# Storing the first batch's g early and lending its place in SBUF to q and v of every second group of four heads

## The chip, the cores and the metric

The kernel runs on one core of a Trainium2 chip. The metric is the time of one execution on the device in microseconds (us), taken as the median of several runs. The profile shows one execution. Its engines are PE (TensorE, matmuls, and PEld for the loading of their weights), DVE (VectorE), ACT (ScalarE), POOL (GpSimd) and SP (SyncE, which here only issues transfers). DMA stands for the 16 engines that carry out the transfers.

## The reference, cut to what matters

```python
def reference(q, k, v, w_a, w_b, w_out, phi, w1, w2):   # q, k, v: (4, 12, 448, 64)
    scores = np.matmul(q, k.transpose(0, 1, 3, 2)) / np.sqrt(64) - np.log(448)
    x = np.matmul(1 / (1 + np.exp(-scores)), v)          # sigmoid attention
    x = x.transpose(0, 2, 1, 3).reshape(1792, 768)
    x = (x @ w_a) * (x @ w_b) @ w_out                    # g = (x @ w_a) * (x @ w_b): 1792 x 1536
    logits = x @ phi                                     # 1792 x 32
    d = softmax(logits, axis=0)                          # over the tokens
    c = softmax(logits, axis=1)                          # over the slots
    s = (d.T @ x).reshape(8, 4, 768)                     # 4 slots for each of 8 experts
    s = [np.maximum(s[e] @ w1[e], 0) @ w2[e] for e in range(8)]
    return c @ np.concatenate(s)
```

## The kernel before

The work is staged as follows. Attention runs over groups `g` of two heads, 24 in all, six to a batch. While PE works on the attention of the second batch, it also forms g of the first batch (`ab(0)`). Then comes the attention of the third and fourth batches alone (groups 12 to 23), with the preparation of the later operands between its steps. Next, g of the second and third batches is formed together in 12 units of seven matrix products (L826), and then g of the fourth batch (`ab(3)`). Last, the expert weights (`e<-in_moe_w`) are streamed in and the experts are computed.

From group `GQ` = 14 on, a head's 448 rows of keys are split into three chunks of 128 and a tail of 64. The tails of an even group and of the odd group behind it are done together, so groups 14 and 15, 16 and 17, 18 and 19, 20 and 21, 22 and 23 each make one group of four heads. For each group:

- SP loads k and q (four transfers each, L141) and v (two transfers, L150 and L151).
- VectorE transposes k (L179), casts it to a high part (L171), subtracts to get a low part (L172) and keeps the tail (L198), and then does the same with q. This is `emit_TK(g)`, and it stands in the program one group ahead of its use.
- PE forms the scores of a chunk in three thirds: high times high, low times high, high times low (L231). ScalarE takes the sigmoid (L237).
- PE multiplies by v (`emit_PV`, L266), and for an odd group also does the tails: their scores (L246) and their product with v (L273).
- The result is copied out (`emit_x`, L296).

Within the loop of group g the order on PE is: the scores of chunk 0 of group g, the product with v of group g-1, then the remaining scores of group g. Three places in SBUF for k, four for q and three for v serve all groups in turn.

The first batch's g is needed in token order for d.T @ g. For its first two thirds (`gi` 0 and 1) VectorE transposes blocks of 32 x 32 into `gk_01`, the result is stored to DRAM (`gk32`, `store_gk`, four transfers for each third, L615) and read back in token order (`reload_gk`, L629 and L630). In this kernel the generator `turn_0` does this late: it takes one step for each step of the attention loop once group 19 is done. The products of `dg` (L919) read what was reloaded.

The order on every engine is that of the program. SP issues its transfers strictly in order, so a transfer that has to wait for its place, or for another transfer, holds all behind it. `load_u` (L694) is a load of weights for the units; its data go through `prep_u`.

Of the kernel before, what the change touches and what calls it, by code (L numbers as in the profile page):

```python
# [9 lines left out]
F32 = mybir.dt.float32  # L10
# [8 lines left out]
B, H, S, D = 4, 12, 448, 64  # L19
DM, FF, NS, NE, F = 768, 1536, 32, 8, 1024  # L20
C = 4
# [9 lines left out]
GQ = 2 * NP + 2  # L31
# [5 lines left out]
def body(ctx, tc, q, k, v, w_a, w_b, w_out, phi, w1, w2, out):  # L37
# [17 lines left out]
    run = {}  # L55
# [22 lines left out]
    gk_01 = lgp.tile([128, 2, 2048], F32, name="gk_01")  # L78
# [38 lines left out]


    qkv_t = {}
    held = []  # L120

    def chunks_of(g):
        return (T, C) if g < GQ else (128, 3)
# [1 line left out]
    def load_qkv(g, names):  # L125
        if g >= B * NP:
            return
        if g > 2 * NP and "raws" not in run:
            held.append((g, names))
            return  # L130
        b, p = divmod(g, NP)
        for src, nm, n in ((k, "k", 3), (q, "q", 4), (v, "v", 3)):
            if nm not in names:
                continue

            t = atp.tile([128, 2 * C * D], F32, tag=nm + "n", name=nm + "n", bufs=n)
            if g >= GT0:
                if nm != "v":
                    t = t[:, :S].rearrange("p (n d) -> p n d", d=32)
                    for j in range(4):  # L140
                        sp.dma_start(out=t[32 * j:32 * j + 32],  # L141
                                     in_=src[b, 2 * p + j // 2][:, j % 2 * 32:j % 2 * 32 + 32].rearrange(
                                         "(n t) d -> t n d", t=32))
                elif g < GQ:
                    t = t[:T].rearrange("p (h c d) -> p h c d", h=2, c=C)
                    sp.dma_start(out=t, in_=src[b, 2 * p:2 * p + 2].rearrange("h (c p) d -> p h c d", c=C))
                else:
                    t = t.rearrange("p (h n) -> p h n", h=2)
                    s, r = src[b, 2 * p:2 * p + 2], 64 * (g % 2)
                    sp.dma_start(out=t[:, :, :192], in_=s[:, :384].rearrange("h (p c) d -> p h (c d)", c=3))  # L150
                    sp.dma_start(out=t[r:r + 64, :, 192:], in_=s[:, 384:].rearrange("h p d -> p h d"))  # L151
                    t = t.rearrange("p h (c d) -> p h c d", c=C)
                qkv_t[nm, g] = t
                continue
            s = src[b, 2 * p:2 * p + 2].rearrange(
                "h (c p) d -> p h c d" if nm == "q" else "h (p c) d -> p h c d", c=C)
            if nm == "v":
                t = t[:T].rearrange("p (h c d) -> p h c d", h=2, c=C)
                sp.dma_start(out=t, in_=s)
            else:  # L160
                t = t[:T].rearrange("p (c h d) -> p c h d", c=C, h=2)
                for h in range(2):
                    (sp if g or not h else act).dma_start(out=t[:, :, h], in_=s[:, h])
            qkv_t[nm, g] = t
# [23 lines left out]
    def emit_TK(g):  # L188
        if g >= B * NP:
            return  # L190
        if g >= GT0:
            for nm in "kq":
                t = transposed(g, nm)
                split_heads(g, nm, t, dve.tensor_copy)
                if g >= GQ:
                    if nm == "k":
                        kr = atp.tile([128, 64], F32, tag="kr", name="kr", bufs=3)
                        dve.tensor_copy(kr, t[:, 384:])  # L198
                        t = kr
                    whole[nm, g] = t  # L200
                if nm == "k" or g <= GQ:
                    load_qkv(g + 3, nm)
            return
        tk = transposed(g, "k")
        if not g:
            tq = transposed(g, "q")
        split_heads(g, "k", tk, dve.tensor_copy)
        if not g:
            split_heads(g, "q", tq, act.copy)
# [30 lines left out]
    def emit_S_rest(g):  # L240

        sc = [ms() for _ in range(2)]
        for d in range(2):
            for h in range(2):
                r, f = slice(64 * h, 64 * h + 64), 64 * d
                pe.matmul(sc[h][f:f + 64], whole["k", g - 1 + d][r], whole["q", g - 1 + d][r], start=True, stop=True)  # L246
        for h in range(2):
            sigmoid(g, h, 3, sc[h], 128)
        for d in range(2):
            del whole["k", g - 1 + d], whole["q", g - 1 + d]  # L250
            load_qkv(g + 3 + d, "q")

    pv_t = {}

# [35 lines left out]
    def emit_x(g):  # L290
        pv = pv_t.pop(g)
        qkv_t.pop(("v", g))
        b, kk = divmod(g, NP)
        if b:
            xt[g] = raw_x(b, kk)
            (dve.tensor_copy if g > GQ and g % 2 else act.copy)(xt[g], pv)  # L296
        else:
            xh = x0p.tile([128, S], F32R, tag=f"xh{kk}", name=f"xh{kk}")
            xl = x0p.tile([128, S], F32R, tag=f"xl{kk}", name=f"xl{kk}")
            act.activation(xh, pv, AF.Copy)  # L300
            dve.tensor_tensor(xl, pv, xh.bitcast(F32), op=ALU.subtract)
            xt[g] = (xh, xl)
        if g < GQ or g % 2 == 0:
            load_qkv(g + 3, "v")

    def att():

        emit_TK(0)
        yield 860
        for g in range(B * NP + 1):  # L310
            more = g < B * NP
            dense = g < NP or g >= 2 * NP
            first = ((0, 1) if g in (0, B * NP - 1) else (0,) if dense else ()) if more else ()
            if g:
                emit_TK(g + 1)
                if g > GQ + 1 and g % 2:
                    load_qkv(g + 1, "v")
                yield 430
            for c in first:
                emit_S(g, (c,))  # L320
                run["done"] = True
                yield 800
            if g:
                if g < NP and more:
                    emit_TQ(g + 1)
                    yield 430
                emit_PV(g - 1)
                if g <= GQ:
                    emit_x(g - 1)
                elif g % 2 == 0:  # L330
                    emit_x(g - 2)
                    emit_x(g - 1)
                yield 3200
            else:
                emit_TK(g + 1)
                yield 430
            if not more:
                return
            if not dense:
                emit_S(g, (0, 1))  # L340
                yield 1600
                emit_TQ(g + 1)
                yield 430
                emit_S(g, (2, 3))
                yield 1600
            else:
                if not g:
                    emit_TQ(g + 1)
                    yield 430
                for c in range(chunks_of(g)[1]):  # L350
                    if c not in first:
                        emit_S(g, (c,))
                        yield 800
                if g >= GQ and g % 2:
                    emit_S_rest(g)
                    yield 800
# [208 lines left out]
    def group(b, gi, evac=(act.copy, dve.tensor_copy) * 2):  # L565
# [12 lines left out]
        if gi < 2:  # L578
            turned = gk[:, :4 * S].rearrange("p (n f) -> p n f", f=128)
            for j in range(4):  # L580
# [3 lines left out]
                    yield  # L584
                gT.pop((b, 4 * gi + j))
                live.discard(b * KF + 4 * gi + j)
            if b:
                yield from store_gk(b, gi, turned)
            else:
                turned_0.append(turned)  # L590
            return
# [17 lines left out]

    turned_0 = []  # L610

    def store_gk(b, gi, turned):
        dst = gk32[b, gi].rearrange("(n t) (r f) -> r t n f", t=32, r=4)
        for r in range(4):
            (act if b == B - 1 else sp).dma_start(out=dst[r], in_=turned[32 * r:32 * r + 32])  # L615
            if b in (0, B - 1):
                yield

    def turn_0():
        for gi in range(2):  # L620
            yield from store_gk(0, gi, turned_0[gi])
        for gi in range(2):
            reload_gk(0, gi, gk_01[:, gi])
            yield

    def reload_gk(b, gi, t):
        t = t.rearrange("p (c n) -> p c n", c=C)
# [467 lines left out]
        next(bg)  # L1095

    base = att_state[0]
    for frac in ab(0):
        att_to(base + NP * PAIR * min(1.0, frac * 1.02))
    att_pairs(2 * NP)  # L1100
    for kk in range(NP):
# [2 lines left out]
    x0_ctx.close()  # L1104
    pools["cp"] = cp_ctx.enter_context(tc.tile_pool(name="cp", bufs=1, side="left"))
    run["lsd2"] = pools["cp"].tile([128, 2 * S + 2 * C * NS], F32, name="ls_d")
    ops, pu, t0 = operands(), None, turn_0()
    wait = [(15, 0), (17, 1)]
    for cost in att_g:
        if wait and wait[0][0] in xt:  # L1110
            load_u(wait.pop(0)[1])
        if 19 in xt:
            next(t0, None)
        if not run.pop("trans", False):
            fill_step()
        run.pop("done", None)
        if next(ops, 0) == 0:
            pu = pu or prep_u(0)
            next(pu, None)
        if (4 * NP - 1, 0, C - 1) in a_t:  # L1120
            break
    run.pop("exp")()
    for _ in t0:
        pass
    for _ in ops:
        pass
    for _ in pu or prep_u(0):
# [198 lines left out]
```

## Time and profile before

| what | value |
|---|---|
| median of 3 runs | 678.41 us (677.24 to 678.56) |
| the profiled execution's own time | 675.91 us |
| its span | 674.1 us |
| PE busy | 634.4 us (94% of the span) |
| DVE busy | 403.6 us (60%) |
| POOL busy | 307.6 us (46%) |
| ACT busy | 283.2 us (42%) |
| moved by DMA | 154.25 MB, 229 GB/s in the mean |

The span is what the profile covers, from the first to the last instruction; the execution's own time includes what lies around it. Busy times are sums over stages with different limits, so the table says how the engines stand to each other, and not which stage could be shorter.

### The profile page before, as it was taken

Reading aid. Unit: us, or ns where it says so; the run is one execution under the profiler, and the core shown is the slowest. Engines: PE = TensorE matmul, PEld = TensorE weight load, DVE = VectorE, ACT = ScalarE, POOL = GpSimd, SP = SyncE. Lnnn points to the kernel's source line nnn. Section 1 sums busy time; section 2 is a strip of 40 time slices with the busy share of each in tenths; the row PEclk is TensorE's granted clock in tenths of the full one; section 3 lists DMA queues with packets and bytes.
Section 4 is the critical chain, followed back from the end, with each engine's and each line's share of the span. In section 5 each row is a group of like instructions: output and inputs, shape, how many; then the busy total and the mean of one; then the engine's idle time right before and its main releaser. Section 6 shows DMA issues by size and latency. Waiting matters only on the chain.

```text
span 674.1 us, 10877 instructions
## 1 busy us (share of the span) xinstructions
PE 634.4 (94%) x4015; PEld 449.8 (67%) x4015; DVE 403.6 (60%) x578; ACT 283.2 (42%) x512; POOL 307.6 (46%) x236
## 2 busy tenths in 40 slices
PE   6999999999998998989999999999999998997585
PEld 4556777777765554559989898898879896442121
DVE  4676899999973889658876777754233323200013
ACT  4888778779644676653332223201110002110022
POOL 0243676676734247549996575742344442000000
PEclk9999999999999999999999999999999999998998
DMA  9998999998863487921123233341999999999998
GB/s 210 272 261 212 292 300 290 307 285 272 263 156 88 86 143 152 238 63 47 48 89 94 71 92 100 96 125 44 294 385 358 403 341 353 404 416 416 410 372 305
DMA packets 145396, 154.25 MB, mean 229 GB/s; under 512 B 74336, under 2 KB 121792, under 8 KB 142272
## 3 DMA queue, kind: packets, MB, share of 16 engines
q1 hardware_dynamic: 138768, 150.01, 72.1%
q10 hardware_dynamic: 6576, 3.56, 1.8%
q8 instruction: 32, 0.52, 0.3%
q14 instruction: 20, 0.16, 0.1%
HBM read 126.36 MB, written 27.17 MB: 228 GB/s over the span
## 4 chain that ended last, share of the span: by engine, by line
PE 72%; DMA 14%; DVE 6%; ACT 3%; issue 1%; SPq 1%; POOL 1%; ACTq 0%; DVEq 0%; POOLq 0%
PE ab L643 23%; PE sc L826 15%; DMA e<-in_moe_w 8%; PE ab L826 7%; PE sc L231 6%; PE sc L260 5%; PE ab L266 3%; DMA vn<-in_v 2%; PE ms L183 2%; PE ms L919 2%; DVE gk L428 1%; DMA gkp<-in_moe_w 1%; PE ms L559 1%; POOL w L433 1%; ACT a L237 1%
## 5 line engine op out<-in xcount | busy, mean ns | idle before, releaser
L433 POOL TENSOR_TENSOR w<-gk,cy 128x768 int32<-128x768 int32 x36 | 66.0, 1835 | 92.8 <-DVE gk L428 51.4
L237 ACT ACTIVATE a<-sc,sums 112x448 f32<-112x448 f32 (+1 forms) x147 | 82.6, 642 | 22.3 <-PE sc L231 21.9
L643 PE MATMUL ab<-t,wh 128*128 128x448 f32 x288 | 65.2, 371 | 0.0
L643 PEld LDWEIGHTS ab<-t,wh 128*128 128x128 f32 x288 | 53.3, 188 | 6.3 <-issue 1.3
L529 POOL TENSOR_TENSOR wl<-wr,wh 128x768 fp32r<-128x768 f32 x16 | 29.4, 1840 | 50.9 <-DVE wh L528 26.5
L650 ACT COPY misc<-ab 128x448 f32<-128x448 f32 x24 | 12.8, 534 | 83.3 <-PE ab L643 76.4
L529 POOL TENSOR_TENSOR wl<-w,wh 128x768 fp32r<-128x768 f32 x24 | 45.0, 1876 | 2.5 <-ACT wh L528 2.5
L1252 PE MATMUL ab<-e,gk 128*32 128x384 f32 x240 | 33.2, 530 | 10.5 <-DMA e<-in_moe_w 10.4
L653 DVE TENSOR_TENSOR misc<-misc,ab 128x448 f32<-128x448 f32 x24 | 14.7, 614 | 42.9 <-PE ab L643 42.9
L260 PE MATMUL sc<-a,vn 112*64 112x448 f32 x192 | 39.1, 546 | 1.0 <-ACT a L237 1.0
L426 DVE TENSOR_SCALAR mf<-gk 128x768 f32<-128x768 f32 x36 | 33.7, 937 | 6.3 <-ACT gk L415 6.2
L707 POOL TENSOR_TENSOR wx<-T,wx 128x384 fp32r<-128x384 f32 x23 | 24.6, 1068 | 24.6 <-ACT wx L706 18.1
L231 PE MATMUL sc<-qh,kh 64*112 64x448 f32 (+1 forms) x147 | 34.7, 444 | 0.7 <-ACT qh L171 0.6
L643 PE MATMUL ab<-xh,wl 128*128 128x448 f32 x144 | 34.4, 374 | 0.9 <-POOL wl L529 0.9
L427 DVE TENSOR_SCALAR gk<-mf 128x768 uint32<-128x768 uint32 x36 | 34.3, 953 | 1.2
L643 PE MATMUL ab<-xh,wh 128*128 128x448 f32 x144 | 34.9, 377 | 0.0
L643 PE MATMUL ab<-xl,wh 128*128 128x448 f32 x144 | 34.5, 375 | 0.0
L1299 DVE COPY o<-sc 128x384 f32<-128x384 f32 x10 | 5.4, 555 | 48.4 <-PE sc L1278 47.2
L643 PE MATMUL ab<-t,wl 128*128 128x448 f32 x144 | 34.2, 373 | 0.0
L706 ACT CAST wx<-T 128x384 fp32r<-128x384 f32 x21 | 10.8, 513 | 55.6 <-DVE T L728 39.0
L707 POOL TENSOR_TENSOR wx<-wr,wx 128x384 fp32r<-128x384 f32 x29 | 32.3, 1114 | 3.7 <-ACT wx L706 3.7
L1252 PEld LDWEIGHTS ab<-e,gk 128*32 128x32 f32 x240 | 9.5, 117 | 32.9 <-DMA e<-in_moe_w 21.5
(478 smaller groups left out, 1512.8 us busy)
## 6 DMA issues: line engine op xcount, KB each, us to landing
e<-in_moe_w SPq DMA_DIRECT2D x23, 1024.0 KB, 8.8
e<-in_moe_w SPq DMA_DIRECT2D x23, 768.0 KB, 15.1
wr<-ab SPq DMA_DIRECT2D x14, 768.0 KB, 4.8
ab<-w SPq DMA_DIRECT2D x24, 384.0 KB, 7.5
gk<-gk SPq DMA_DIRECT2D x24, 224.0 KB, 3.9
e<-in_moe_w SPq DMA_DIRECT2D x14, 384.0 KB, 8.8
wr_cv<-in_moe_w_a SPq DMA_DIRECT2D x6, 768.0 KB, 7.6
wr_all<-in_moe_w_b SPq DMA_DIRECT2D x6, 768.0 KB, 7.2
```

The lines of the kernel that those rows point to most:

```text
L231: pe.matmul(sc[h], kx[r, cs], qx[r], start=(i == 0), stop=(i == 2))
L237: act.activation(a, sc, AF.Sigmoid, bias=nlog[:n], scale=1.0 / math.sqrt(D))
L260: pe.matmul(pv[64 * h:64 * h + 64], qkv_t["v", g][:, h, c, :], a_t.pop((g, h, c)), start=(c == 0), stop=(c == C - 1))
L266: pe.matmul(pv[64 * h:64 * h + 64], qkv_t["v", g][:, h, c], a_t.pop((g, h, c)), start=(c == 0), stop=False)
L426: dve.tensor_scalar(mf, m, LOW, HIGH, op0=ALU.max, op1=ALU.min)
L427: dve.tensor_scalar(mi, mf.bitcast(U32), 3, 0x3FFFFFFF, op0=ALU.logical_shift_left, op1=ALU.bitwise_and)
L433: pool.tensor_tensor(thirds(w), m.bitcast(I32), thirds(cy_t.pop(x)), op=ALU.add)
L529: pool.tensor_tensor(wl, t, wh.bitcast(F32), op=ALU.subtract)
L643: pe.matmul(t, w[:, kk * 128:(kk + 1) * 128], xt[b * NP + kk][xi], start=(s == 0 and kk == 0), stop=(s == 2 and kk == KD - 1))
L707: pool.tensor_tensor(w[:, 1], t, w[:, 0].bitcast(F32), op=ALU.subtract)
L826: pe.matmul(t, w[:, wi, k * 128:(k + 1) * 128], xs[ORDER[m], k][xi], start=(s == 0 and k == 0), stop=(s == 2 and k == 2))
L1252: pe.matmul(sps[h][32 * j:32 * j + 32], hT[:, 2 * x + i, 2 * j + g], ring[order2[n + j]][0][:, i, c0:c0 + w], start=(g == 0 and x == 0 and ...
```

## The change

The stores of the first batch's g are issued inside `ab(0)`, at its steps 66 and 69 of 72, instead of late in the attention loop. From then on the two halves of `gk_01` hold, in eight pieces of 512 columns, q and v of groups 16 and 17 (second half) and of groups 20 and 21 (first half). The groups 14, 15, 18, 19, 22 and 23 keep the ordinary places, of which q now has three. With the places spread so, the calls of `load_qkv` for q and v stand earlier in the program. Loads that are asked for before the stores are kept in `aside` and issued right behind them. The reload of the second half is asked for after group 19's result, that of the first half after group 21's; `load_u(1)` goes between them.

```diff
@@ load_qkv
-        for src, nm, n in ((k, "k", 3), (q, "q", 4), (v, "v", 3)):
+        for src, nm, n in ((k, "k", 3), (q, "q", 3), (v, "v", 3)):
             if nm not in names:
                 continue
 
-            t = atp.tile([128, 2 * C * D], F32, tag=nm + "n", name=nm + "n", bufs=n)
+            if nm != "k" and g >= GQ and (g - GQ) // 2 % 2:
+                if "stored" not in run:
+                    aside.append((g, nm))
+                    continue
+                i = 4 * (g < GQ + 4) + 2 * (nm == "v") + g % 2
+                t = small[:, 512 * i:512 * (i + 1)]
+            else:
+                t = atp.tile([128, 2 * C * D], F32, tag=nm + "n", name=nm + "n", bufs=n)
@@ emit_TK
-                if nm == "k" or g <= GQ:
+                if nm == "k" or g not in (GQ + 2, GQ + 6):
                     load_qkv(g + 3, nm)
@@ emit_S_rest
         for d in range(2):
             del whole["k", g - 1 + d], whole["q", g - 1 + d]
-            load_qkv(g + 3 + d, "q")
+        if g in (GQ + 1, GQ + 5):
+            load_qkv(g + 4, "q")
@@ emit_x
-        if g < GQ or g % 2 == 0:
+        if g < GQ:
             load_qkv(g + 3, "v")
+        if g >= GQ - 1 and g % 2:
+            load_qkv(g + 4, "v")
@@ att
                 emit_TK(g + 1)
-                if g > GQ + 1 and g % 2:
-                    load_qkv(g + 1, "v")
+                if g > GQ and g % 2:
+                    load_qkv(g + 3, "v")
@@ store_gk
-    def store_gk(b, gi, turned):
+    def store_gk(b, gi, turned, eng=sp, rows=range(4)):
         dst = gk32[b, gi].rearrange("(n t) (r f) -> r t n f", t=32, r=4)
-        for r in range(4):
-            (act if b == B - 1 else sp).dma_start(out=dst[r], in_=turned[32 * r:32 * r + 32])
-            if b in (0, B - 1):
-                yield
-
-    def turn_0():
-        for gi in range(2):
-            yield from store_gk(0, gi, turned_0[gi])
-        for gi in range(2):
-            reload_gk(0, gi, gk_01[:, gi])
-            yield
+        for r in rows:
+            eng.dma_start(out=dst[r], in_=turned[32 * r:32 * r + 32])
@@ the main program
-    for frac in ab(0):
+    for i, frac in enumerate(ab(0)):
+        if i in (66, 69):
+            store_gk(0, i // 69, turned_0[i // 69])
+            if i == 69:
+                run["stored"] = True
+                for a in aside:
+                    load_qkv(*a)
         att_to(base + NP * PAIR * min(1.0, frac * 1.02))
...
-    ops, pu, t0 = operands(), None, turn_0()
-    wait = [(15, 0), (17, 1)]
+    ops, pu = operands(), None
+    then = [(GQ + 1, lambda: load_u(0)), (GQ + 5, lambda: reload_gk(0, 1, gk_01[:, 1])),
+            (GQ + 6, lambda: load_u(1)), (GQ + 7, lambda: reload_gk(0, 0, gk_01[:, 0]))]
     for cost in att_g:
-        if wait and wait[0][0] in xt:
-            load_u(wait.pop(0)[1])
-        if 19 in xt:
-            next(t0, None)
+        if then and then[0][0] in xt:
+            then.pop(0)[1]()
```

The change moves transfers on SP's queue. The first place is the end of `ab(0)`. Before, SP's queue runs from the load of k of group 16 as follows: q of group 16, v 14, k 17, q 17, v 15, k 18, v 16, a store of logits, and k 19.

```order
L141 DMA kn_2323<-in_k 32x14x32 x4
L141 DMA qn_2333<-in_q 32x14x32 x4
L150 DMA vn_2379<-in_v 128x2x192
L151 DMA vn_2379<-in_v 64x2x64
L141 DMA kn_2505<-in_k 32x14x32 x4
L141 DMA qn_2515<-in_q 32x14x32 x4
L150 DMA vn_2556<-in_v 128x2x192
L151 DMA vn_2556<-in_v 64x2x64
L141 DMA kn_2624<-in_k 32x14x32 x4
L150 DMA vn_2663<-in_v 128x2x192
```

After the change SP's queue at the same place runs so, again from k of group 16; `gk32_102<-gk_01_93` are the stores, and `gk_01_93<-in_q` and `gk_01_93<-in_v` load q and v of groups 16 and 17 into their place.

```order
L148 DMA kn_2323<-in_k 32x14x32 x4
L629 DMA gk32_102<-gk_01_93 32x14x128 x4
L157 DMA vn_2378<-in_v 128x2x192
L158 DMA vn_2378<-in_v 64x2x64
L629 DMA gk32_102<-gk_01_93 32x14x128 x4
L148 DMA gk_01_93<-in_q 32x14x32 x4
L148 DMA kn_2512<-in_k 32x14x32 x4
L148 DMA gk_01_93<-in_q 32x14x32 x4
L157 DMA vn_2562<-in_v 128x2x192
L158 DMA vn_2562<-in_v 64x2x64
L148 DMA kn_2630<-in_k 32x14x32 x4
L148 DMA qn_2640<-in_q 32x14x32 x4
```

The eight stores now stand between k 16 and k 17, q 16 behind them, and q 18 has come forward to k 18.

The second place is the end of the attention loop. Before, SP's queue ends it with the second set of q for groups 22 and 23, v 21, three stores, v 22, five stores, the two reloads (L629 and L630 twice), and last v 23.

```order
L141 DMA qn_3103<-in_q 32x14x32 x4
L150 DMA vn_3156<-in_v 128x2x192
L151 DMA vn_3156<-in_v 64x2x64
L615 DMA gk32_102<-gk_01_93 32x14x128 x3
L150 DMA vn_3204<-in_v 128x2x192
L151 DMA vn_3204<-in_v 64x2x64
L615 DMA gk32_102<-gk_01_93 32x14x128 x5
L629 DMA gk_01_93<-gk32_102 128x3x512
L630 DMA gk_01_93<-gk32_102 64x512
L629 DMA gk_01_93<-gk32_102 128x3x512
L630 DMA gk_01_93<-gk32_102 64x512
L150 DMA vn_3306<-in_v 128x2x192
```

After the change SP's queue ends that loop with k 23, v 22, q 23, v 23, the reload of the second half, the load of weights for the second unit (L699), and the reload of the first half.

```order
L148 DMA kn_3032<-in_k 32x14x32 x4
L157 DMA vn_3042<-in_v 128x2x192
L158 DMA vn_3042<-in_v 64x2x64
L148 DMA qn_3107<-in_q 32x14x32 x4
L157 DMA vn_3162<-in_v 128x2x192
L158 DMA vn_3162<-in_v 64x2x64
L634 DMA gk_01_93<-gk32_102 128x3x512
L635 DMA gk_01_93<-gk32_102 64x512
L699 DMA wr_3299<-ab32_99 128x2x768
L634 DMA gk_01_93<-gk32_102 128x3x512
L635 DMA gk_01_93<-gk32_102 64x512
```

The stores are gone from here, and v 23 has moved from behind both reloads to ahead of them. On PE, VectorE, ScalarE and GpSimd the order of instructions is the same before and after; some of them read q and v from `gk_01` instead of `qn` and `vn`.

## Rows read from the trace of the kernel before

**Rows 1.** Stretches: length; busy PE, PEld, DVE, ACT, POOL; PE clock; DMA share; GB/s
```profile
253.00:293.10 40.10, 34.99 (x218) 17.35 (x216) 26.78 (x38) 24.39 (x45) 21.97 (x20) 0.96 0.82 190
293.10:484.00 190.90, 190.90 (x1099) 167.71 (x1095) 131.47 (x189) 54.82 (x120) 125.29 (x108) 1.00 0.32 90
484.00:655.00 171.00, 154.07 (x1144) 96.30 (x1136) 36.53 (x71) 15.93 (x34) 34.06 (x30) 0.98 1.02 384
```

**Rows 2.** Chain of waits in order of time: start us, us, what
```profile
260.69 6.20 DMA vn<-in_v
...
281.81 7.82 DMA vn<-in_v
```

**Rows 3.** PE timeline: start us, us, instruction, count [idle before, releaser]
```profile
259.51 2.48 PE L266 MATMUL ab<-a,vn 128*64 128x448 f32 x12 [0.48 <-DMA vn<-in_v]
...
267.02 4.17 PE L266 MATMUL ab<-a,vn 128*64 128x448 f32 x12 [2.02 <-DMA vn<-in_v]
...
273.53 0.54 PE L231 MATMUL sc<-qh,kh 64*128 64x448 f32 x2
...
274.41 2.48 PE L266 MATMUL ab<-a,vn 128*64 128x448 f32 x12
276.81 0.98 PE L273 MATMUL ab<-a,vn 64*64 64x448 f32 x8
...
289.76 2.48 PE L266 MATMUL ab<-a,vn 128*64 128x448 f32 x12 [2.61 <-DMA vn<-in_v]
...
299.10 1.11 PE L919 MATMUL ms<-gk,ls_d 128*32 128x128 f32 x28
```

**Rows 4.** Table of stretches, PE alone: us, busy (x), clock, DMA share, GB/s
```profile
268.00:269.00 1.00, 1.00 (x6) 0.50 0.68 105
...
288.00:289.00 1.00, 0.00 (x0) 1.00 1.03 327
```

**Rows 5.** Timeline of SP's queue
```profile
205.79 1.99 SPq L141 DMA_DIRECT2D qn<-in_q  x4
...
208.35 0.67 SPq L151 DMA_DIRECT2D vn<-in_v  x1
218.02 1.89 SPq L141 DMA_DIRECT2D kn<-in_k  x4
...
268.95 2.05 SPq L615 DMA_DIRECT2D gk<-gk  x3
...
273.37 4.47 SPq L615 DMA_DIRECT2D gk<-gk  x5
```

**Rows 6.** DMA issues by line, whole span: size of one, median us to landing
```profile
gk<-gk SPq DMA_DIRECT2D x24, 224.0 KB, 3.9
...
gk<-gk SPq DMA_DIRECT2D x4, 768.0 KB, 8.0
...
gk<-gk ACTq DMA_DIRECT2D x8, 224.0 KB, 9.5
```

**Rows 7.** Timeline of VectorE
```profile
181.70 0.64 DVE L581 STREAM_TRANSPOSE gk<-misc 128x448 f32<-128x448 f32 x1
...
235.08 0.39 DVE L171 CAST kh<-kn 128x448 fp32r<-128x448 f32 x1 [1.16 <-PE sc L231]
...
237.27 0.63 DVE L172 TENSOR_TENSOR ql<-qn,qh 128x448 fp32r<-128x448 f32 x1
...
265.54 1.16 DVE L171 CAST kh<-kn 128x448 fp32r<-128x448 f32 x1
...
270.24 1.30 DVE L172 TENSOR_TENSOR ql<-qn,qh 128x448 fp32r<-128x448 f32 x1
...
272.76 0.39 DVE L171 CAST kh<-kn 128x448 fp32r<-128x448 f32 x1 [0.66 <-PE sc L231]
```

**Rows 8.** Timeline of GpSimd
```profile
266.42 1.14 POOL L707 TENSOR_TENSOR wx<-wr,wx 128x384 fp32r<-128x384 f32 x1
267.51 1.37 POOL L720 TENSOR_TENSOR T<-wr 128x384 f32<-128x384 f32 x1
```

More of the change, by code (lines that the diff above doesn't have):

```diff
@@ L119, in body @@
     qkv_t = {}
-    held = []
+    held, aside = [], []
     def chunks_of(g):
@@ L586, in group @@
                 live.discard(b * KF + 4 * gi + j)
-            if b:
-                yield from store_gk(b, gi, turned)
+            if b == B - 1:
+                for r in range(4):
+                    store_gk(b, gi, turned, act, (r,))
+                    yield
+            elif b:
+                store_gk(b, gi, turned)
             else:
@@ L1122, in body @@
     run.pop("exp")()
-    for _ in t0:
-        pass
     for _ in ops:
```

## The prediction

> **What bounds the kernel now.** I began with the table of stretches [rows 1]. The reader should set the PE column against the length of each stretch, and then look at the DMA share. From 484 to 655 the DMA share is 1.02: the expert weights stream in without a pause, and TensorE waits inside that stretch. From 293.1 to 484 PE is busy for all of 190.9 us. Between 253 and 293.1 it is busy 34.99 of 40.1 us at a clock of 0.96, and this is the stretch that the change touches: attention for the last groups of heads. The weight stream begins as PE frees places in SBUF, and the 190.9 us ahead of it hold no idle time. So a microsecond won before 293 starts everything behind it a microsecond earlier, and should arrive whole at the end.
>
> The chain of waits says what PE lacked there [rows 2]: it leaves PE for loads of v, one of 6.20 us from 260.69 and one of 7.82 us from 281.81. The PE timeline gives the price [rows 3]. The product with v (L266) sat idle 0.48 us before 259.51 (group 19), 2.02 before 267.02 (group 20) and 2.61 before 289.76 (group 23), together 5.11, which is the 40.1 less 34.99 of [rows 1]. Group 20's product then took 4.17 us where group 21's took 2.48: at 268 the granted clock was 0.50, that is 1.2 GHz, after PE had stood still for 2.02 us [rows 4]. That is another 1.69. After the 2.61 us the clock stayed at 1.00. The whole loss is 5.11 + 1.69 = 6.8 us.
>
> Why v comes late is read from SP's queue [rows 5]. The eight stores of the first batch's g sit there (L615, three from 268.95 and five from 273.37, 2.05 + 4.47 us of issuing), ahead of two reloads, and the load of v 23 is issued behind both, at 281.81 [rows 2]. The loads of v 19 and v 20 are asked for one or two groups before their use, and stand behind the loads of k and q.
>
> **The change part by part.** *The loads.* v 18 to v 23 are asked for about two groups earlier. In the new order of SP's queue v 20 stands right behind k 21 and q 21, and v 23 ahead of the reloads. One group takes (274.41 - 259.51 - 2.02 - 1.69) / 2 = 5.6 us on PE [rows 3], so the lead is some 11 us, and the longest v load of the chain took 7.82. v 23 uses the place of v 18, free after the tails of group 19: 259.51 + 2.48 + 0.98 gives 263 as its earliest issue, and even 7.82 us later, at 271, it is far ahead of its use. I take the three waits on v as gone. Bounds: 0 of the 5.11 if the queue holds v up again, all of it if not. The number of loads is unchanged.
>
> *The stores.* They move to SP's queue behind the load of k 16, to 205.79, where q 16 was issued. Their data is ready: the last transposition that writes them is at 181.70 [rows 7]. From 208.35 + 0.67 to 218.02 SP issued nothing [rows 5]. Eight stores at 0.8 us (6.52 / 8) and two issues of v take the queue to about 213.4, and q 16, now into the stored place, must wait until its store has landed. A store lands in 3.9 us in the middle [rows 6], so that wait ends near 217.3, and it costs nothing since the load of k 17 behind it did not go before 218.02. Cover: k 17 is cast by VectorE at 235.08 [rows 7], so SP could be held some 12 us more. At the slowest landing shown, 9.5 us on the other queue, k 17 goes at about 224 and still hides.
>
> *The reloads.* The second half is read back once v 23 is asked for, with nothing to wait for. The first half must wait for the tails of group 21, which end at 276.81 + 0.98 = 277.8 before and at 275.3 after the shift worked out below. A reload lands in 8.0 us [rows 6], hence near 283.3. The first products with g start at 299.10 before [rows 3], at 294 after the shift, so 10 us of cover remain. One load of the next weights (L694) moves behind the first reload; its readers belong to the second unit, behind those products. Both cost nothing.
>
> *The rest.* On PE, VectorE, ScalarE and GpSimd the sequence of instructions is the same; the operands' places alone differ. One place fewer for q costs nothing, as the three left serve groups 14 to 15, 18 to 19 and 22 to 23 in turn.
>
> *What is late next.* Without the waits PE would reach the scores of group 22 at 273.53 - (0.48 + 2.02 + 1.69) = 269.34. They need group 22's k and q split on VectorE, and there the last subtraction runs from 270.24 to 271.54 [rows 7]. VectorE had no pause in this piece; the next is the 0.66 before 272.76, which PE caused. No load holds it either, so it won't be earlier. The scores take 274.41 - 273.53 = 0.88 in three thirds; the last third, which needs that subtraction, goes at about 271.6, and the product of group 21 at 271.9 instead of 274.41. Of the first 4.19 us only 2.5 come back. Behind it VectorE is in time: for group 23, 272.76 + 2.82 (group 17's pace, next paragraph) less the 0.66 that falls away is 274.9, and it is wanted only after group 21's product and tails, at 271.9 + 2.48 + 0.98 = 275.4. From there everything is 2.5 us earlier until the idle 2.61 ahead of group 23's product, which falls away whole. The sum is 2.5 + 2.6 = 5.1 us.
>
> The term rests on VectorE staying slow. From the start of the cast of k to the end of the subtraction of q, group 22 takes 6.00 us (265.54 to 271.54) and group 17 took 2.82 (235.08 to 237.90) [rows 7]. At the fast pace group 22 would be ready at 268.4, PE would not wait, and the gain would be the whole 6.8. In the slow piece GpSimd runs one instruction right behind the other, as from 266.42 to 268.88 [rows 8], and the change moves none of them: they follow VectorE's own results. Between the two paces I take the slow one, since its row is that of this very piece. The Trainium skill, "SBUF — State Buffer", section "SBUF: two separate sides", says that VectorE (in its two-port modes or with two inputs) and GpSimd share a pair of ports as an exclusive lock, and that the one that comes second waits out the other's whole instruction. By that rule the stretched times are waits for a GpSimd that will be as busy after the change, and the sum is 5.1; by VectorE's bare durations it would be 6.8. The trace agrees: the cast of k is 0.39 us at 235.08, and 1.16 at 265.54 beside a GpSimd instruction.
>
> **The rivals.**
> *The clock falls again.* In the new timeline PE stands still for 271.6 - 269.34 less two thirds of 0.88, about 1.7 us, in two pieces with four matmuls between. Before, 2.02 us of standing were followed by 1.2 GHz, and 2.61 were not [rows 3, 4]. If it falls, the product of group 21 takes 4.17 instead of 2.48, and the gain is 5.1 - 1.7 = 3.4: 675.0 us. The break between makes it the less likely.
> *VectorE is no bound.* If the contention falls otherwise and group 22 is ready by 269.7, the gain is 6.8: 671.6 us. Against it stands that nothing that feeds VectorE or GpSimd moves.
> *The gain is lost behind.* If the weight stream from 484 on does not follow PE, or another load is late, between nothing and 2 us is left: 676.4 to 678.4. Against it speaks the DMA share of 0.32 before 484 [rows 1]: the stream can start earlier.
> *Slower.* SP is held at q 16 by the stores, and k 17 comes late for VectorE. SP must be free by about 231 with no loss, and each microsecond of hold beyond that is one lost in the scores. To eat the 5.1 us and be measurably slower it must stay held until about 238, that is, the stores would have to take 25 us to land. At 27 us (free at 240) the time would be 678.4 - 5.1 + 9 = 682. They took 3.9, at worst 9.5 [rows 6].
>
> **How the numbers follow.** The profiled execution took 675.91 us, 1.8 more than its span of 674.1; less 5.1 it is 670.8, with a span of 669.0. The median of the runs, 678.41, lies 0.4% above that execution; I put the prediction against the median: 678.41 - 5.1 = 673.3 us. Chances: 5.1 us within 0.8 either way 0.55 (672.5 to 674.1), clock 0.17, VectorE free 0.10, lost behind 0.12, slower 0.06. 0.2% (1.35 us) is about what a measurement of this kernel can tell from no change. Faster: 0.55 + 0.17 + 0.10 and a quarter of "lost behind" = 0.85; no change, the rest of that case, 0.09; slower 0.06. The range takes in both the 6.8 and the 3.4 with 0.6 to 1.0 us for the spread of the runs (677.24 to 678.56): 671.0 to 676.0. It leaves out most of the last two cases.
>
> **What would show it.** In the profile after: no wait of L266 on a v load; a wait of PE on VectorE before the scores of group 22, some 1.7 us, and VectorE's last subtraction there still near 271.5; SP issuing the stores from 206 to 213 and the load of k 17 at 218; the reload landed 10 us before the first products with g; these starting near 294, and 375 us (674.1 - 299.1) from there to the end. I am wrong if L266 still waits for v, if the scores of group 22 don't wait, if the clock is 0.5 after that wait, or if those 375 us grow.

## The result and the profile after

| | before | after |
|---|---|---|
| median of the runs | 678.56 us (677.24 to 680.19, 5 runs) | 669.64 us (668.87 to 674.30, 5 runs) |
| the profiled execution's own time | 675.91 us | 669.15 us |
| its span | 674.1 us | 667.4 us |

The ratio is 0.988, with a 95% interval of 0.9841 to 0.9919: faster by 8.9 us in this comparison. The prediction said 673.3 (671.0 to 676.0), so the change brought more than the range allowed. The direction is right, and the profile shows the forecast wait for VectorE almost to the tenth. Yet the predicted gain was 5.1 us, and it has to be found out where the rest comes from.

The table of stretches of the kernel after answers to [rows 1]. Its columns are: stretch and length; busy time (and count) of PE, PEld, DVE, ACT and POOL; PE clock; DMA share; GB/s.

```profile
253.00:293.10 40.10, 38.42 (x252) 21.65 (x252) 31.00 (x45) 29.35 (x57) 24.40 (x22) 1.00 0.52 133
293.10:484.00 190.90, 190.90 (x1126) 167.12 (x1115) 129.31 (x188) 48.66 (x107) 123.59 (x107) 1.00 0.36 103
484.00:655.00 171.00, 153.47 (x1129) 94.13 (x1127) 37.13 (x72) 18.32 (x39) 32.26 (x29) 0.98 1.00 381
```

PE is busy 38.42 of 40.1 us where it had 34.99, its clock is 1.00 throughout, and the DMA share fell from 0.82 to 0.52, mainly since the eight stores are gone from here (8 x 224 KB are 1.8 of the 2.3 MB that the stretch moves less). The 1.68 us that are left idle stand in the PE timeline of the kernel after (start us, us, instruction, count, idle before and releaser), which answers to [rows 3]; L274 is now the product with v and L238 are the scores.

```profile
257.59 2.48 PE L274 MATMUL ab<-a,vn 128*64 128x448 f32 x12
263.02 2.48 PE L274 MATMUL ab<-a,gk 128*64 128x448 f32 x12
269.06 0.54 PE L238 MATMUL sc<-qh,kh 64*128 64x448 f32 x2 [1.17 <-DVE qh L178]
270.32 0.53 PE L238 MATMUL sc<-ql,kh 64*128 64x448 f32 x2 [0.51 <-DVE ql L179]
270.78 2.48 PE L274 MATMUL ab<-a,gk 128*64 128x448 f32 x12
...
283.46 2.48 PE L274 MATMUL ab<-a,vn 128*64 128x448 f32 x12
285.86 0.98 PE L281 MATMUL ab<-a,vn 64*64 64x448 f32 x8
...
292.81 2.36 PE L924 MATMUL ms<-gk,ls_d 128*32 128x128 f32 x64
```

None of the products of groups 19, 20, 21 and 23 waits for v any more. In place of that, PE waits 1.17 + 0.51 = 1.68 us for VectorE ahead of group 22's scores. The last VectorE row of that split, which answers to [rows 7], ends at 268.95 + 1.31 = 270.26, and the cast that begins it is as slow as before. The prediction had the end near 271.5; with the 1.39 us by which this profile runs ahead from 203 us on (below) it is 271.65. The timeline of VectorE after:

```profile
264.21 1.17 DVE L178 CAST kh<-kn 128x448 fp32r<-128x448 f32 x1
...
266.65 1.00 DVE L205 COPY kr<-kn 128x64 f32<-128x64 f32 x1
...
268.95 1.31 DVE L179 TENSOR_TENSOR ql<-qn,qh 128x448 fp32r<-128x448 f32 x1
```

The chain of waits of the kernel after answers to [rows 2]; between 253 and 293 it holds no load of v, and leaves PE for VectorE instead.

```profile
264.21 1.18 DVE kh L178
...
268.95 1.32 DVE ql L179
270.85 2.40 PE ab L274 x12
```

The timeline of SP's queue after answers to [rows 5]. L629 are the stores, L148 loads of q and k, L157 loads of v, L634 the reloads.

```profile
204.35 3.22 SPq L629 DMA_DIRECT2D gk<-gk  x4
...
209.98 3.94 SPq L629 DMA_DIRECT2D gk<-gk  x4
214.01 3.53 SPq L148 DMA_DIRECT2D gk<-in_q  x4
217.60 2.03 SPq L148 DMA_DIRECT2D kn<-in_k  x4
...
265.29 0.42 SPq L157 DMA_DIRECT2D vn<-in_v  x1
...
266.40 1.45 SPq L634 DMA_DIRECT2D gk<-gk  x1
...
274.22 0.36 SPq L634 DMA_DIRECT2D gk<-gk  x1
```

The stores end at 213.92, q 16 behind them takes 3.53 us to issue (the profile counts only 0.2 us of that as a wait for a store), and k 17 goes at 217.60, where it went at 218.02 before. v 23 is asked for at 265.29, 18 us ahead of its product, and the last reload at 274.22, 18.6 us ahead of the first product with g; it lands 5.0 us later.

So far nothing explains more than 5.1 us. Lining up the two timelines by the same instruction does. From 140 to 200 us the kernels are less than 0.2 us apart (before that up to 0.7). Then come these rows of the PE timeline, of the kernel before:

```profile
203.14 0.87 PE L458 MATMUL ms<-ident,w 128*128 128x128 f32 x6 [1.39 <-POOL w L433]
204.91 1.48 PE L643 MATMUL ab<-xh,wl 128*128 128x448 f32 x6 [0.89 <-POOL wl L529]
```

and of the kernel after:

```profile
201.75 0.87 PE L468 MATMUL ms<-ident,w 128*128 128x128 f32 x6 [0.18 <-POOL w L443]
203.52 1.48 PE L648 MATMUL ab<-xh,wl 128*128 128x448 f32 x6 [0.90 <-POOL wl L539]
```

Here PE waits for GpSimd, which waits for a transfer of prepared weights. That wait was 1.39 us before and 0.18 after, and it ends ahead of the first transfer that the change moves, the stores from 204.35. Behind it the stage from this matmul to the first product with g takes 299.10 - 204.91 = 94.19 us before and 292.81 - 203.52 = 89.29 after. That is 4.90 us, against 5.1 predicted. From there to the end of the span it is 375.0 and 374.6. With the 204.91 - 203.52 = 1.39 us near 203 the sum is 1.39 + 4.90 + 0.4 = 6.7 us, as between the spans. The medians' 8.9 us are 2.2 more than that.

**The theories.** Theory A: the change is worth some 5 us, as in the stage, and the rest is the spread of single runs, which the first few runs showed too small. Rival B: what stands near 203 us belongs to the change too, and it is worth nearly 9. For where the 5 us come from: theory C, both edits count, the earlier loads of v and the moved stores. Its rival D: the wait for v 23 alone carries the gain, since VectorE's wait of 1.7 us takes the place of what the other loads give back. And on VectorE: theory E, GpSimd's instructions beside it stretch the split. (Each quoted expectation below letters its own theories; only A and B of the first two, A of the last and D of v_early_2 are the ones named here.)

### The profile page after: what moved, and what is told of

Its sections match the earlier page's. It is cut to its first block, busy times and chain, and to the rows that moved or that the text cites. A ratio compares the mean times of both kernels' runs of the same rounds, so it can differ in the third digit from the quotient of the medians.

```text
span 667.4 us, 10895 instructions
## 1 busy us (share of the span) xinstructions
PE 632.0 (95%) x4015; PEld 448.7 (67%) x4015; DVE 403.9 (61%) x578; ACT 283.5 (42%) x512; POOL 309.2 (46%) x236
## 4 chain that ended last, share of the span: by engine, by line
PE 69%; DMA 16%; DVE 5%; ACT 3%; SPq 2%; issue 2%; POOL 1%; ACTq 0%; DVEq 0%; POOLq 0%
PE ab L648 21%; PE sc L831 16%; DMA e<-in_moe_w 8%; PE ab L831 7%; PE sc L238 5%; PE sc L268 4%; DMA out<-w 3%; PE ab L274 2%; SPq L148 2%; DMA ab<-w 2%; PE ms L924 2%; PE ms L190 2%; DMA gkp<-in_moe_w 1%; PE ms L569 1%; ACT a L244 1%
## 5 line engine op out<-in xcount | busy, mean ns | idle before, releaser
L238 PE MATMUL sc<-qh,kh 64*112 64x448 f32 (+1 forms) x147 | 34.7, 444 | 1.9 <-DVE qh L178 1.2
L711 ACT CAST wx<-T 128x384 fp32r<-128x384 f32 x21 | 10.8, 513 | 55.7 <-DVE T L733 39.0
```

What stands on the lines that cost most here:

```text
L238: pe.matmul(sc[h], kx[r, cs], qx[r], start=(i == 0), stop=(i == 2))
```

## The experiments

The runs came in two sets, each with its own runs of the kernel before: 23 with a median of 676.36 us (670.72 to 680.84), and 30 with a median of 674.51 us (669.38 to 679.27). Ratios are to the runs of before in the same set.

### before_again and after_again: the two kernels once more (first set)

No edit in either.

> The kernel before, unchanged, timed against itself. Theory A (the change is worth 4.9 us by its own mechanism, and the rest of the 8.9 us between the medians is spread from run to run): this kernel lies within 1.5 us of itself, single runs spread over some 3 us, and in this profile PE reaches the transpositions of w near the end of the first batch's g (before at 203.14 us, after at 201.75) at a time of its own, up to 1.5 us away from 203.14. Rival B (the 1.4 us there come from the change): PE is there within 0.3 us of 203.14 again.

> The changed kernel, unchanged. Theory A: 4 to 7 us faster than before (ratio 0.990 to 0.994), and PE reaches the transpositions of w somewhere between 201 and 204 us. Rival B: 8 to 9 us faster again (ratio 0.987 to 0.988), and PE there at 201.8 within 0.3.

Measured: before_again 677.53 us (672.47 to 679.08, 12 runs), ratio 1.0014 (0.9986 to 1.0042), as the same kernel must. after_again 672.14 us (668.12 to 675.73, 12 runs), ratio 0.9924 (0.9897 to 0.9951), which is 5.1 us. The PE timeline of before_again shows the old waits with other sizes than [rows 3]:

```profile
256.66 2.48 PE L266 MATMUL ab<-a,vn 128*64 128x448 f32 x12 [0.36 <-DMA vn<-in_v]
263.84 2.48 PE L266 MATMUL ab<-a,vn 128*64 128x448 f32 x12 [1.69 <-ACT a L237]
...
269.54 2.48 PE L266 MATMUL ab<-a,vn 128*64 128x448 f32 x12
...
286.79 4.12 PE L266 MATMUL ab<-a,vn 128*64 128x448 f32 x12 [4.52 <-DMA vn<-in_v]
```

Group 20's product loses 1.69 us without a fall of the clock (the clock is 1.00 from 264 to 276). The row names ScalarE. But the load of v 20, issued at 257.62, landed 6.1 us later, at 263.7, some 0.1 us ahead of the product, as in [rows 2, 3] (266.89 and 267.02). And in the kernel after the same product starts 1.1 us behind the start of these sigmoids, here 2.8 us. So this, too, is read as a wait for v 20. Group 23's product waits 4.52 us instead of 2.61, and this time the clock falls there, to 0.50: the product takes 4.12 us. What the change removes is thus not the same in each execution. Near 203 before_again starts the matmul at 202.17 and after_again at 202.50: the kernel before was the earlier one here, so the difference of 1.39 us in the first pair of profiles is no effect of the change. Rival B falls by that. Theory A's own numbers were too small: the 12 runs of before lie over 6.6 us and not over 3, and the transpositions of w start at 200.71, 2.4 us from 203.14 and not at most 1.5.

### stores_only: the kernel before with the stores moved alone (first set)

```diff
@@ store_gk
-            if b in (0, B - 1):
+            if b == B - 1:
                 yield
@@ turn_0
-        for gi in range(2):
-            yield from store_gk(0, gi, turned_0[gi])
+        for _ in range(8):
+            yield
@@ the main program
-    for frac in ab(0):
+    for i, frac in enumerate(ab(0)):
+        if i in (66, 69):
+            for _ in store_gk(0, i // 69, turned_0[i // 69]):
+                pass
```

> The kernel before with only the stores of the first batch's g moved to the steps 66 and 69; four places for q, three for v, all loads and reloads asked for where they were. Theory A (group 19 and 20 wait because their v is asked for late, group 23 because its v shares the DMA engines and the queue with stores and reloads): the waits before groups 19 and 20 stay (0.5 and 2.0 us, and perhaps the low clock behind), the wait before group 23 falls from 2.6 us to under 1; gain 2 to 3 us. Rival C (the stores in the queue make all three waits): all three are gone, gain near 5 us.

Measured: 670.05 us (669.37 to 673.52, 6 runs), ratio 0.9918 (0.9887 to 0.995), that is 5.5 us: the whole gain and not a part of it. Its PE timeline:

```profile
258.98 2.48 PE L266 MATMUL ab<-a,vn 128*64 128x448 f32 x12 [1.15 <-DMA vn<-in_v]
265.03 2.48 PE L266 MATMUL ab<-a,vn 128*64 128x448 f32 x12 [0.55 <-ACT a L237]
...
283.60 2.48 PE L266 MATMUL ab<-a,vn 128*64 128x448 f32 x12
```

The places of v and their loads are the old ones, and groups 19 and 20 still lose 1.15 + 0.55 = 1.70 us. (The second row names ScalarE, but the load of v 20, issued at 260.78, landed 4.1 us later, at 264.9, as above some 0.1 us ahead of the product.) But group 22's scores then find VectorE ready, where the kernel after waits 1.68 us. Both kernels pay the same once. v 23 still stands behind both reloads, but SP no longer has the stores ahead of them: the load is issued at 274.37, right after group 21's tails have freed its place, and lands in 6.1 us, ahead of the product at 283.60. In the kernel before the place was free at 277.8 and the load went at 281.81; in before_again at 272.9 and 279.78. So of the quoted expectation the waits came as its theory A said and the gain as its rival C said, since neither reckoned with VectorE's wait. Theory C as named above falls for these profiles; D fits. How far the waits ahead of it weigh is seen from the matmul near 203 to group 21's product: 67.26 us in the kernel after, 67.24 here, 67.37 in before_again, and 69.50 in the first profile of before, where the clock's fall at group 20 alone is 1.69.

### v_early and v_early_2: the loads of v earlier, the stores left late (first and second set)

Two v tiles go into 512 columns of `gk_01` that are free in the kernel before, so that v can be asked for as early as in the kernel after.

```diff
@@ load_qkv
-            t = atp.tile([128, 2 * C * D], F32, tag=nm + "n", name=nm + "n", bufs=n)
+            tail = nm == "v" and g in (17, 21)
+            t = gk_01[:, :, 1792:] if tail else atp.tile([128, 2 * C * D], F32, tag=nm + "n", name=nm + "n", bufs=n)
...
@@ emit_x
-        if g < GQ or g % 2 == 0:
+        if g < GQ:
             load_qkv(g + 3, "v")
+        if g >= GQ - 1 and g % 2:
+            if g >= GQ:
+                load_qkv(g + 3, "v")
+            load_qkv(g + 4, "v")
@@ att
-                if g > GQ + 1 and g % 2:
-                    load_qkv(g + 1, "v")
```

v_early_2 also lets the reloads come four steps of the attention loop later, which is the only difference between the two:

```diff
@@ turn_0
             yield from store_gk(0, gi, turned_0[gi])
+        for _ in range(4):
+            yield
         for gi in range(2):
```

> The kernel before with the loads of v 17 to v 23 asked for one or two groups earlier (v 17 and v 21 into the 512 columns of the place of g that its transposed form leaves free); the stores stay late, q stays as before. Theory A: the three v waits are gone although the stores are late, PE waits for VectorE before the scores of group 22 instead, some 1.7 us; gain 4 to 5.5 us, as with the whole change. Rival C (the stores are what holds the queue): the wait before group 23 or 22 stays, gain under 2.5 us.

In v_early the reload stands, in program order, ahead of the last use of v 21 and overwrites it, so group 21's product is formed with other data, and has to wait for the reload. Measured: 689.1 us, ratio 1.0185 (1.0148 to 1.0221); 13.80 us of idle time in PE's timeline ahead of that product, at 284.65, are the price of this order. It says nothing on the stores. Up to there it has no wait for v, and the same two waits for VectorE (1.16 and 0.50) as the kernel after.

> The kernel before with v 17 to v 23 asked for one or two groups earlier (v 17 and v 21 in the 512 columns that the transposed g leaves free), the reloads four steps later so that they stand behind the last use of v 21, and the stores late in the queue as before. Theory D (the stores on the queue and the DMA engines cost only the wait before group 23; once v 23 stands ahead of them they cost nothing): no wait on v, some 1.7 us of waiting for VectorE at the scores of group 22, gain 4 to 5.5 us. Rival E (stores and reloads so late hurt whatever the loads do): a wait appears elsewhere, at the first products with g, for the reload, of 2 us or more, and the gain is under 3 us.

Measured: 671.11 us (668.87 to 676.69, 12 runs), ratio 0.9965 (0.9933 to 0.9996), between 0.3 and 4.5 us. Its PE timeline:

```profile
270.58 0.54 PE L232 MATMUL sc<-qh,kh 64*128 64x448 f32 x2 [1.15 <-DVE qh L172]
271.84 0.53 PE L232 MATMUL sc<-ql,kh 64*128 64x448 f32 x2 [0.51 <-DVE ql L173]
...
284.96 2.48 PE L267 MATMUL ab<-a,vn 128*64 128x448 f32 x12
```

With the stores still late, but v 23 asked for ahead of them, the waits are those of the kernel after, and the stage takes 89.27 us (294.32 - 205.05), as there. So in this profile the stores cost nothing by themselves; what costs is that v 23 stands behind them. Either order that takes v 23 out of that place gives the stage of the kernel after. D is shown in the profiles, one for each edit. The timed gain does not decide it: its middle, 2.4 us, is under the 4 to 5.5 that theory D gave and inside rival E's "under 3", though the wait for the reload that E asked for is not there.

### after_pool_late and stores_pool_late: GpSimd's instructions moved out of VectorE's way (second set)

Theory E is tested by letting the first preparation of weights, whose subtractions on GpSimd stand beside group 22's split, come four steps later. The edit also takes the VectorE cast that feeds them (0.35 us) from ahead of the split to behind it. It is put on the kernel after and on stores_only alike.

```diff
@@ prep_u
+        if not u:
+            for _ in range(4):
+                yield
         block(u, 0, b11)
...
             eng.tensor_tensor(t4, b21, t2, op=ALU.subtract)
-            for _ in range(8):
+            for _ in range(4):
                 yield
```

> The changed kernel, with the first preparation of weights on GpSimd (one cast on VectorE and five GpSimd instructions that follow it) moved four steps later, behind VectorE's split of group 22. Theory A (VectorE's split of group 22 is slow because GpSimd works beside it, and it is what PE waits for in the changed kernel): the split from the cast of k to the last subtraction of q falls from 6.0 us to some 3.5 to 4.5, the two waits of 1.15 and 0.51 us before the scores of group 22 vanish, and PE's first products with g come 1.5 us earlier than in the changed kernel. Rival: VectorE's durations stay as they are, and so do the waits.

Measured: 666.9 us (666.33 to 669.25, 7 runs), ratio 0.9896 (0.9857 to 0.9935), the lowest median here. The kernel after had 670.52 in the same set (after_third, below), but the intervals overlap, so the size of the gain is taken from the profile. GpSimd's timeline has the gap that the edit makes:

```profile
263.15 1.16 POOL L766 TENSOR_TENSOR t<-t,s 128x448 f32<-128x448 f32 x1
267.31 1.02 POOL L712 TENSOR_TENSOR wx<-wr,wx 128x384 fp32r<-128x384 f32 x1 [3.00 <-DVE wx L711]
```

and VectorE's timeline shows group 22's split in it:

```profile
263.16 1.40 DVE L178 CAST kh<-kn 128x448 fp32r<-128x448 f32 x1
264.59 0.62 DVE L179 TENSOR_TENSOR kl<-kn,kh 128x448 fp32r<-128x448 f32 x1
265.13 0.19 DVE L205 COPY kr<-kn 128x64 f32<-128x64 f32 x1
...
266.34 0.63 DVE L179 TENSOR_TENSOR ql<-qn,qh 128x448 fp32r<-128x448 f32 x1
```

The first cast, still beside a GpSimd instruction, takes 1.40 us. From 264.31 GpSimd stands still, and VectorE's rows fall to 0.62, 0.19 and 0.63, where the subtractions took 1.31 in the kernel after. From the first cast to the end of the last subtraction it is 3.81 us instead of 270.26 - 264.21 = 6.05. PE no longer waits ahead of group 22's scores; 0.29 us remain ahead of group 23's. The stage takes 290.17 - 202.75 = 87.42 us, 1.87 less than in the kernel after.

By the Trainium skill, "SBUF — State Buffer", section "SBUF: two separate sides", an instruction of VectorE in a two-port mode, or with two inputs, and one of GpSimd (against two inputs, one that reads SBUF) exclude each other for their whole length. The rows agree: same VectorE instructions, same data sizes, 1.31 us beside GpSimd and 0.62 or 0.63 without it.

> The kernel with only the stores moved, and the same preparation on GpSimd four steps later. Theory A (late v before groups 19 and 20 and VectorE's late split of group 22 lie in parallel, and whichever is later counts): the waits on v before groups 19 and 20 stay, some 1.5 to 2.5 us, and the time is that of the kernel with the stores moved alone, within 1 us; only with v early does the late preparation pay. Rival: it gains 1.5 us here too.

Measured: 669.08 us (667.1 to 672.07, 12 runs), ratio 0.9924 (0.9898 to 0.9951). Its PE timeline:

```profile
260.51 2.48 PE L266 MATMUL ab<-a,vn 128*64 128x448 f32 x12 [0.37 <-DMA vn<-in_v]
267.76 2.48 PE L266 MATMUL ab<-a,vn 128*64 128x448 f32 x12 [1.75 <-DMA vn<-in_v]
...
286.13 2.48 PE L266 MATMUL ab<-a,vn 128*64 128x448 f32 x12
```

Here the wait for v is still there, 0.37 + 1.75 = 2.12 us, and VectorE's speed gives nothing: the stage is 89.5 us without a slower clock near 203 (worked out in the last part of this section), against 89.26 in stores_only. The same edit is worth 1.87 us in the stage where v is early, and nothing where v is late. The two waits lie side by side, and only whoever removes both is paid. This is where the earlier loads of v 19 and v 20 earn something.

### after_third: the kernel after in the second set

No edit.

> The changed kernel once more, on the same chip as the three others, as their measure. Theory A: 4 to 5.5 us faster than before, with the two waits for VectorE of together 1.7 us before the scores of group 22 and no wait on v.

Measured: 670.52 us (667.44 to 674.77, 12 runs), ratio 0.9943 (0.9915 to 0.9972), which is 3.8 us (1.9 to 5.7), just under the 4 to 5.5 expected. Its profiled execution, of 673.25 us, is one of the slower, and its PE timeline shows two reasons:

```profile
203.09 0.88 PE L468 MATMUL ms<-ident,w 128*128 128x128 f32 x6 [1.94 <-POOL w L443]
204.86 2.61 PE L648 MATMUL ab<-xh,wl 128*128 128x448 f32 x6 [0.89 <-POOL wl L539]
...
271.92 0.54 PE L238 MATMUL sc<-qh,kh 64*128 64x448 f32 x2 [1.15 <-DVE qh L178]
273.17 0.74 PE L238 MATMUL sc<-ql,kh 64*128 64x448 f32 x2 [0.51 <-DVE ql L179]
273.84 3.75 PE L274 MATMUL ab<-a,gk 128*64 128x448 f32 x12
```

Near 203 PE waits 1.94 us instead of 0.18, and the six matmuls behind it take 2.61 us instead of 1.48. After the waits for VectorE the clock falls to 0.50, and group 21's product takes 3.75 instead of 2.48.

### The profiles side by side

Each span is cut at the matmul behind the wait near 203 us and at the first product with g (the times are starts in the PE timelines; v_early is left out).

| profile | start near 203 | from there to the first product with g | from there to the end | span |
|---|---|---|---|---|
| before | 204.91 | 94.19 | 375.0 | 674.1 |
| before_again | 202.17 | 95.61 | 374.4 | 672.2 |
| after | 203.52 | 89.29 | 374.6 | 667.4 |
| after_again | 202.50 | 89.28 | 374.5 | 666.3 |
| after_third | 204.86 | 92.28 | 374.4 | 671.5 |
| stores_only | 203.69 | 89.26 | 374.7 | 667.6 |
| v_early_2 | 205.05 | 89.27 | 374.7 | 669.0 |
| stores_pool_late | 204.43 | 91.05 | 374.3 | 669.8 |
| after_pool_late | 202.75 | 87.42 | 374.3 | 664.5 |

The first column varies by 2.9 us with no order by kernel. SP's queue shows where that begins, ahead of every transfer that the change moves: the load of q (four transfers) near 182 us takes 5.08 to 5.74 us to issue in the four profiles with the latest starts (204.43 to 205.05) and 3.29 to 3.68 in the other five. Both sorts occur with the order before and the order after; what holds the load is not known. The middle column is where the edits act. Two rows of it also hold a slower clock right behind the wait near 203: the next group of the same matmuls, 3.62 us later in the kernel after, starts 5.14 us later in after_third and 5.19 in stores_pool_late. Without those 1.5 and 1.6 us, and without the 1.3 + 0.2 of group 21 in after_third, both stand at 89.3 and 89.5, beside the others.

## Why the prediction missed, step by step

**The waits on v vanish: right.** All three are gone in each profile of the kernel after.

**What is late next: right, in place and size.** PE was to wait about 1.7 us for VectorE's split of group 22; it waits 1.68, 1.66 and 1.66 in the three profiles. VectorE's sequence is as slow as before (6.05 us, before 6.00). The rival in which VectorE is no bound did not come, and after_pool_late shows its mechanism and its price: 1.87 us in the stage, where 6.8 - 5.1 = 1.7 had been worked out.

**The sum of 5.1 us: right in the profile.** The stage became 4.9 us shorter in the first pair of profiles. By the second profile of before it would be 95.61 - 89.28 = 6.3, since there the clock fell at group 23 and v 23 was 4.52 us late. Timed again, the change gave 5.1 and 3.8 us. The first products with g start at 292.81, or 294.2 with the 1.39 us near 203 added (predicted 294), and from there to the end it is 374.6 us (predicted 375). All runs together have medians of 676.0 (70 of before, 669.38 to 680.84) and 670.7 (29 of after, 667.44 to 675.73), 5.3 us apart, though the sets differ.

**The stores, q 16 and the reloads: right.** k 17 went at 217.60 (predicted 218), the stores from 204.35 to 213.92 (206 to 213), and no reader waits for a reload. The rival in which it becomes slower needed SP held until 238; it was free at 217.5.

**The clock falls again: right as a rival.** It was given 0.17 and appears in one of three profiles, with a price of 1.3 us at the product (1.7 predicted) and 0.2 at the scores ahead of it.

**How the numbers follow: the step that failed.** The median that it started from was too high for this kernel, and its spread too narrow. It put the prediction "against the median: 678.41 - 5.1 = 673.3 us" and gave the spread of the runs 0.6 to 1.0 us, from three runs between 677.24 and 678.56. The same step had the other figure too: against the profiled execution "it is 670.8", and the median of all 29 runs of after is 670.7. (That the profiled execution lay so near the middle, 675.91 against 676.0, is luck.) The three runs were a high and narrow draw: of 70 runs of before, 26 lie above 677.2, and the whole lies over 11.5 us. Nor can 0.2% (1.35 us) be told, as the same step held: the three intervals for the change are 3.7 to 5.3 us wide. The first comparison drew before high (678.56) and after a little low (669.64), and made 8.9 us out of some 5; its interval (5.5 to 10.8 us) and those of the two later ones (3.3 to 7.0 and 1.9 to 5.7) have 5.5 to 5.7 us in common. The profiles show where such a spread can come from: the wait near 203 us (0 to 2.0 us, and up to 1.6 more where the clock falls behind it), the landing of v 23 (2.61 or 4.52 us late), and the place where the clock falls (group 20, group 23, group 21 or nowhere). That the first runs differ by just these is argued, not shown, since only one execution of each has a profile. Whether the chip on which they ran adds something also stays open.

**What the prediction credited to the earlier loads: too much.** It let 2.5 of the 5.1 us come back in the first part, for v 19 and v 20. That is what the profile of before gives, where the clock happened to fall at group 20. Where it doesn't fall, as in stores_only, the late loads cost 1.70 us, which VectorE's wait costs anyway. Against before_again, too, the kernel after is only 0.11 us ahead up to group 21's product. There the place of v 23 behind the stores carries the rest alone, its wait of 4.52 us and the slower clock behind it (4.12 - 2.48 = 1.64); in the first profile of before it is 2.61 of the 4.9 us.

## What to carry to other kernels

When a wait is removed, look for what runs beside it: here the load of v and VectorE's split were late by the same 1.7 us, one edit alone earned nothing, and after both the kernel is at 666.9 us. Before trusting a median of three runs, compare it with the profiled execution; if they differ by more than the runs do among themselves (here 2.5 us against 1.3), the spread is larger than shown, and the range must take that in. To find what an edit brought, line the two timelines up by the same instructions and cut the span where the difference jumps, since a jump ahead of the first changed instruction is hardly the edit's; a second profile of each kernel shows whether it is.

## What the runs showed of the hardware

The clock followed no simple account of how long PE stood still. It fell to 1.2 GHz after 2.02 us in [rows 3, 4] and after 4.52 us in before_again, and not after 2.61 us in the same first profile. Behind the two waits for VectorE, of 1.68, 1.66 and 1.66 us, it fell once in three profiles of the same kernel. Near 203 us it fell behind waits of 1.94 and 0.89 us (after_third) and of 2.00 and 0.90 us (stores_pool_late), and not behind 1.61 and 0.89 us (v_early_2). The table of stretches of the kernel after, of PE alone, shows such a wait without a fall:

```profile
268.00:269.00 1.00, 0.00 (x0) 1.00 0.62 45
269.00:270.00 1.00, 0.74 (x4) 1.00 0.63 162
270.00:271.00 1.00, 0.68 (x4) 1.00 1.05 408
```

A VectorE cast of 0.39 us [rows 7] took 1.40 beside a GpSimd instruction, and a copy of 0.19 us took 1.00. A pause of 3.0 us on GpSimd shortened a sequence of six VectorE instructions by 2.2 us (6.05 to 3.81).
